# A decode kernel that streams 178 MB: VectorE looped over attention, waits thinned out, and the front of the kernel loaded in another order

## The chip, the cores and the metric

The kernel runs on one core of one Trainium2 chip. The metric is device time in microseconds (us); a kernel is run several times and medians are quoted. Each run reports a state, fast or slow; all runs used here were fast. Engines are named as in the profile: PE (TensorE), DVE (VectorE), ACT (ScalarE), POOL (GpSimd), SP (SyncE, which issues the loads). "DMA engine" always means one of the 16 engines that move data, never a compute engine.

## The reference

One decode step, batch 2, one new token each, in bfloat16:

```python
mod = (silu(c) @ w_mod).reshape(2, 6, 1, 1024)      # w_mod 1024 x 6144: 12.6 MB
sa, ca, ga, sb, cb, gb = mod
h = layernorm(x) * (1 + ca) + sa
x = x + ga * attention(h, k_cache, v_cache, wq, wo) # 32 query heads, 4 kv heads, 32768 keys of 128
h = layernorm(x) * (1 + cb) + sb
x = x + gb * mlp(h, w1, b1, w2, b2)                 # 1024 -> 3584 -> 1024
```

The two caches are 134 MB of the 178 MB that must be read. Arithmetic is small beside that.

## The kernel before

One queue (SP) issues all loads, mostly of 2 MB, into a 160 KB ring per partition. A block is loaded again as soon as the last reader of the slot is done. K blocks are turned (transposed) by PE into PSUM, evicted by DVE (5 of 8) or ACT (3 of 8), and multiplied with the query; softmax of a (batch, head) pair is one round behind.

A small recording layer, the Tracker, works out which semaphore each instruction must wait for and writes out each engine's program. PE's program is already a loop over the 8 rounds; DVE's and ACT's are written out in full, round after round:

```python
    def _compute_waits(self, E, tokens):
        need = {}
        for key, val in tokens:
            if val > need.get(key, 0):
                need[key] = val
        waits = []
        for key, val in need.items():
            if self.waited.get((E, key), 0) >= val:    # only what this engine itself waited for
                continue
            waits.append((key, val))
            self.waited[(E, key)] = val
        return waits
    # ...
    def _put(self, E, op):
        (self.segment if E == "pe" and self.segment is not None else self.ops[E]).append(op)
```

The parts of the attention that the change touches:

```python
    def tr(i, cc, g8):
        # ... 8 transposes of a K block into psKT[kq] on PE
        if EVAC_PATTERN[g8] == "act":
            act(lambda e, src=src: e.activation(KT_sb[g8][:, :, :], src, ACT.Copy), ...)
        else:
            dve(lambda e, src=src: e.tensor_copy(KT_sb[g8][:, :, :], src), ...)

    def qk(i, cc, g8):
        # ... 8 matmuls into ps
        if g8 == TPC // 8 - 1:
            Sc = S_sb[i % 2][:, :, cc * TPC:(cc + 1) * TPC]
            act(lambda e: e.activation(Sc, ps[:, :].rearrange("p (t h) -> p h t", h=HPG), ACT.Copy), ...)
            dve(lambda e: e.tensor_reduce(m1c[:, :, cc], Sc, AX.X, ALU.max), ...)
```

And the front:

```python
    wm_v = w_mod.rearrange("(k p) n -> p k n", k=KT8)          # block k = 128 lines that follow one another
    # ...
    T.dma("sp", lambda e: e.dma_start(c16[:, :], c.rearrange("b (k p) -> (b k) p", p=128)), ...)   # 16 lines of 256 B
    T.dma("sp", lambda e: e.dma_start(x16[:, :], A_x.rearrange("b o (k p) -> (b o k) p", p=128)), ...)
    # ... c16 and x16 are each turned by one small matmul into psM
```

## Time and profile before

| | before |
|---|---|
| time, median of 3 (lowest to highest) | 425.29 us (425.28 to 425.34) |
| span of the profiled execution | 423.6 us |
| bytes, mean rate | 178.50 MB, 421 GB/s |
| busy PE / DVE / ACT | 72% / 39% / 37% |
| last 2 MB load landed at | 417.75 us |

These lines are from the page of the kernel before: the span, engine busy times, then the DMA rows of the 40 slices (DMA share in tenths, rate in each slice), and the DMA queues (packets, MB, share of the time of all 16 DMA engines).

```profile
span 423.6 us, 11650 instructions
PE 305.5 (72%) x5164; PEld 244.0 (58%) x5164; DVE 167.3 (39%) x347; ACT 157.1 (37%) x269; POOL 4.9 (1%) x23
...
DMA  8999999999999999999999999999999999999994
GB/s 325 428 430 426 433 434 429 419 432 431 430 436 427 435 425 434 430 432 433 428 435 425 434 432 430 435 427 436 425 432 431 432 433 427 432 430 422 427 428 185
...
q1 hardware_dynamic: 14350, 178.29, 98.7%
q8 instruction: 9, 0.15, 0.1%
q14 instruction: 8, 0.07, 0.0%
```

The stream is unbroken from the second slice to the last but one. q1 carries the data, while the two "instruction" queues bring program code to the engines.

From the groups of instructions of the kernel before (busy us, mean ns of one | idle time just before them, and what ended it):

```profile
L507 DVE COPY KT_sb<-psKT 128x1024 bf16<-128x1024 bf16 x160 | 108.5, 690 | 118.1 <-PE psKT L501 117.8
L505 ACT ACTIVATE KT_sb<-psKT 128x1024 bf16<-128x1024 bf16 x96 | 98.0, 1020 | 129.7 <-PE psKT L501 129.3
L518 DVE TENSOR_REDUCE m1c<-S_sb 128x8 f32<-128x512 f32 x32 | 21.9, 685 | 13.6 <-ACT S_sb L517 12.5
```

DVE and ACT stand idle before the evictions for over 100 us each, waiting for PE, which itself waits for data. So they are not what the kernel waits for.

The end of the chain of waits, before (start us, length us, what):

```profile
386.99 30.76 DMA w<-in_B_w_dram
...
417.79 2.87 PE psO L721 x96
420.69 0.19 DVE mT L724
```

And the end of the stream in windows of 1 us, before (the last two columns are the DMA share and GB/s):

```profile
core 0: us, PE busy (x) PEld busy (x) DVE busy (x) ACT busy (x) POOL busy (x), PEclk, DMA share, GB/s
414.00:415.00 1.00, 0.85 (x12) 0.18 (x4) 0.10 (x1) 0.00 (x0) 0.00 (x0) 0.79 1.01 424
415.00:416.00 1.00, 0.35 (x3) 0.35 (x4) 0.60 (x1) 0.00 (x0) 0.00 (x0) 1.00 1.01 424
416.00:417.00 1.00, 0.70 (x7) 0.62 (x6) 0.00 (x0) 0.00 (x0) 0.00 (x0) 1.00 0.86 352
417.00:418.00 1.00, 0.21 (x8) 0.21 (x9) 0.00 (x0) 0.00 (x0) 0.00 (x0) 0.92 0.59 240
418.00:419.00 1.00, 1.00 (x43) 1.00 (x41) 0.00 (x0) 0.00 (x0) 0.00 (x0) 0.50 0.23 88
419.00:420.00 1.00, 1.00 (x38) 0.93 (x36) 0.00 (x0) 0.00 (x0) 0.00 (x0) 0.50 0.12 39
```

The stream does not stop; it fades over some 4 us.

### The profile page before, as it was taken

What the parts mean: (1) busy time and instruction counts of PE and PEld (TensorE: products, weight loads), DVE (VectorE), ACT (ScalarE), POOL (GpSimd) and SP (SyncE); (2) the same over time, 40 slices, a digit from 0 to 9 for tenths busy, and PEclk for the clock granted to TensorE, in tenths of its full rate; (3) what the DMA queues carried; (4) which work ended last, traced back from release to release, by engine and by line L of the source; (5) the groups of instructions that cost most, each with busy time, mean ns of one, the idle gap of its engine ahead of it and who ended that gap; (6) DMA issues with size and microseconds to landing.
All of it is one profiled execution on the core that took longest, in us unless ns stands there. A gap on an engine that the chain in (4) does not pass through costs nothing.

```text
span 423.6 us, 11650 instructions
## 1 busy us (share of the span) xinstructions
PE 305.5 (72%) x5164; PEld 244.0 (58%) x5164; DVE 167.3 (39%) x347; ACT 157.1 (37%) x269; POOL 4.9 (1%) x23
## 2 busy tenths in 40 slices
PE   1546467988997879788877958896878682645575
PEld 0105157976975769677676837785867661212244
DVE  1102025644673464446435524652555343101311
ACT  2000024638555446433733543473438234100020
POOL 3000000000000000000000000000000000000000
PEclk9999859869999886888969898887989886655566
DMA  8999999999999999999999999999999999999994
GB/s 325 428 430 426 433 434 429 419 432 431 430 436 427 435 425 434 430 432 433 428 435 425 434 432 430 435 427 436 425 432 431 432 433 427 432 430 422 427 428 185
DMA packets 14367, 178.50 MB, mean 421 GB/s; under 512 B 1543, under 2 KB 1550, under 8 KB 2830
## 3 DMA queue, kind: packets, MB, share of 16 engines
q1 hardware_dynamic: 14350, 178.29, 98.7%
q8 instruction: 9, 0.15, 0.1%
q14 instruction: 8, 0.07, 0.0%
HBM read 178.28 MB, written 0.00 MB: 421 GB/s over the span
## 4 chain that ended last, share of the span: by engine, by line
DMA 76%; PE 16%; SPq 5%; ACT 1%; issue 1%; DVE 0%; ACTq 0%; DVEq 0%
DMA K<-in_A_k_cache_dram 60%; PE psKT L501 11%; DMA wo<-in_A_wo_dram 8%; DMA w<-in_B_w_dram 7%; SPq L377 5%; PE psS L513 3%; PE psO L543 1%; PE psO L721 1%; ACT KT_sb L505 1%; ACT E_sb L534 0%; PE psS L642 0%; ACT L534 0%; DVE KT_sb L507 0%; PE psM L524 0%; SPq L392 0%
## 5 line engine op out<-in xcount | busy, mean ns | idle before, releaser
L501 PE MATMUL psKT<-ident,K 128*128 128x128 bf16 x2048 | 180.5, 242 | 36.8 <-DMA K<-in_A_k_cache_dram 34.4
L501 PEld LDWEIGHTS psKT<-ident,K 128*128 128x128 bf16 x2048 | 138.8, 109 | 47.9 <-DMA K<-in_A_k_cache_dram 41.1
L507 DVE COPY KT_sb<-psKT 128x1024 bf16<-128x1024 bf16 x160 | 108.5, 690 | 118.1 <-PE psKT L501 117.8
L505 ACT ACTIVATE KT_sb<-psKT 128x1024 bf16<-128x1024 bf16 x96 | 98.0, 1020 | 129.7 <-PE psKT L501 129.3
L513 PE MATMUL psS<-qcur,KT_sb 128*128 128x8 bf16 x2048 | 88.8, 168 | 7.7 <-ACT KT_sb L505 6.5
L513 PEld LDWEIGHTS psS<-qcur,KT_sb 128*128 128x128 bf16 x2048 | 80.7, 100 | 13.1 <-ACT KT_sb L505 8.4
L543 PE MATMUL psO<-V,E_sb 128*32 128x512 bf16 x512 | 35.6, 406 | 1.9 <-DMA V<-in_A_v_cache_dram 1.0
L534 ACT ACTIVATE E_sb<-S_sb,negm 128x256 bf16<-128x256 f32 x64 | 32.3, 504 | 10.9 <-DVE negm L530 10.0
L518 DVE TENSOR_REDUCE m1c<-S_sb 128x8 f32<-128x512 f32 x32 | 21.9, 685 | 13.6 <-ACT S_sb L517 12.5
L517 ACT ACTIVATE S_sb<-psS 128x512 f32<-128x512 f32 x32 | 19.0, 593 | 14.0 <-PE psS L513 13.9
L543 PEld LDWEIGHTS psO<-V,E_sb 128*32 128x32 bf16 x512 | 11.5, 100 | 12.8 <-issue 2.8
L452 PE MATMUL psS<-wmod,inT 128*32 128x512 bf16 x64 | 8.4, 622 | 12.0 <-DMA wmod<-in_w_mod_dram 12.0
L642 PE MATMUL psS<-wo,atT 128*32 128x512 bf16 x64 | 7.6, 627 | 11.9 <-DMA wo<-in_A_wo_dram 11.9
L423 ACT ACTIVATE stat<-stat 128x2 f32<-128x2 f32 x3 | 0.6, 204 | 37.0 <-DVE stat L422 37.0
L473 PE MATMUL psS<-wq,inT 128*32 128x512 bf16 x64 | 7.1, 602 | 7.4 <-DMA wq<-in_A_wq_dram 6.3
L534 ACT ACTIVATION_READ_ACCUMULATOR E_sb<-S_sb,negm 128x1 f32 x64 | 12.1, 189 | 0.0
L452 PEld LDWEIGHTS psS<-wmod,inT 128*32 128x32 bf16 x64 | 1.3, 112 | 18.0 <-DMA wmod<-in_w_mod_dram 17.5
L642 PEld LDWEIGHTS psS<-wo,atT 128*32 128x32 bf16 x64 | 1.9, 128 | 16.6 <-DMA wo<-in_A_wo_dram 14.5
L564 PE MATMUL psM<-msum,hmat 128*128 128x128 f32 x16 | 4.2, 346 | 7.5 <-DVE msum L558 7.5
L458 ACT ACTIVATE S_sb<-psS 128x512 f32<-128x512 f32 x1 | 0.6, 597 | 22.9 <-DVE S_sb L460 22.9
L460 DVE COPY S_sb<-psS 128x512 f32<-128x512 f32 x1 | 0.7, 691 | 20.7 <-PE psS L452 20.7
L558 DVE SCALAR_TENSOR_TENSOR msum<-psO,mk,msum 128x128 f32<-128x128 f32 x24 | 8.4, 351 | 0.9
(115 smaller groups left out, 129.7 us busy)
## 6 DMA issues: line engine op xcount, KB each, us to landing
K<-in_A_k_cache_dram SPq DMA_DIRECT2D x32, 2048.0 KB, 31.4
V<-in_A_v_cache_dram SPq DMA_DIRECT2D x32, 2048.0 KB, 35.2
wmod<-in_w_mod_dram SPq DMA_DIRECT2D x8, 1536.0 KB, 16.6
wq<-in_A_wq_dram SPq DMA_DIRECT2D x4, 2048.0 KB, 37.9
wo<-in_A_wo_dram SPq DMA_DIRECT2D x4, 2048.0 KB, 27.7
w<-in_B_w_dram SPq DMA_DIRECT2D x4, 1792.0 KB, 37.9
w<-in_B_w_dram SPq DMA_DIRECT2D x3, 2048.0 KB, 30.8
w<-in_B_w_dram SPq DMA_DIRECT2D x1, 768.0 KB, 28.6
```

Source lines behind the costliest of these rows:

```text
L377: T.dma("sp", lambda e, dst=dst, src=cur.src: e.dma_start(dst, src), key=cur.sem, writes=[cur.reg], frees=old)
L452: pe(lambda e, w=it.view, k=k, ch=ch, n=n, q=q: e.matmul(bank[n][32 * q:32 * q + 32, :], lhsT=inT[:, k, :], rhs=w[:, ch * 512:(ch + 1) * 512],
L501: pe(lambda e, kq=kq, jj=jj, w=it.view, t=t: e.transpose(psKT[kq][:, jj * 128:(jj + 1) * 128], w[:, t, :], ident[:, :]), reads=[it.reg, "i ...
L505: act(lambda e, src=src: e.activation(KT_sb[g8][:, :, :], src, ACT.Copy), reads=[f"psKT{kq}"], writes=[f"KT_sb{g8}"], sem=f"ev{cc}_{g8}")
L507: dve(lambda e, src=src: e.tensor_copy(KT_sb[g8][:, :, :], src), reads=[f"psKT{kq}"], writes=[f"KT_sb{g8}"], sem=f"ev{cc}_{g8}")
L513: pe(lambda e, t=t, jj=jj: e.matmul(ps[:, t * HPG:(t + 1) * HPG], lhsT=KT_sb[g8][:, jj, :], rhs=qcur[:, :], start=True, stop=True), reads= ...
L517: act(lambda e: e.activation(Sc, ps[:, :].rearrange("p (t h) -> p h t", h=HPG), ACT.Copy), reads=[preg], writes=[f"S_sb{i % 2}_{cc}"], sem ...
L518: dve(lambda e: e.tensor_reduce(m1c[:, :, cc], Sc, AX.X, ALU.max), reads=[f"S_sb{i % 2}_{cc}"], writes=[f"m1c{cc}"])
L534: act(lambda e: e.activation(E_sb[:, :, h, :], S_sb[j][:, h, :].rearrange("p (u t) -> p u t", t=4), ACT.Exp, bias=negm[:, h:h + 1], scale= ...
L543: pe(lambda e, t4=t4, tg=tg, q=q: e.matmul(psO[32 * q:32 * q + 32, :], lhsT=E_sb[:, tg // 4, :, :].rearrange("p h t -> p (h t)"), rhs=it.v ...
L558: dve(lambda e, q=q: e.scalar_tensor_tensor(out=msum[:, :], in0=psO[:, q * 128:(q + 1) * 128], scalar=mk4[:, q:q + 1], in1=msum[:, :], op0 ...
L642: pe(lambda e, w=it.view, g=g, j=j, hf=hf, q=q: e.matmul(psS[0][32 * q:32 * q + 32, :], lhsT=atT[g][:, j, :], rhs=w[:, j, hf * 512:(hf + 1 ...
```

## The change

The Tracker now knows what a wait implies: if the other engine had itself waited for something, so has this one (`_learn`), and that wait is left out. DVE's eight rounds are folded into one loop body as PE's are. For that, each round must use the same addresses, so the running maximum reads PSUM rather than one of two buffers, and GpSimd copies each round's result to its place. The front loads c as two lines of 2 KB and turns it with 8 small matmuls; to match the order in which c then lies, block k of w_mod is every eighth line of the matrix.

```diff
+    LOOPED = ("pe", "dve")
...
+    def _learn(self, E, key, val):
+        known = self.known[E]
+        known[key] = max(known.get(key, 0), val)
+        for v, what in reversed(self.seen[key]):
+            if v <= val:
+                for k, x in what.items():
+                    if x > known.get(k, 0):
+                        known[k] = x
+                break
...
-            if self.waited.get((E, key), 0) >= val:
+            if self.known[E].get(key, 0) >= val:
                 continue
...
-        (self.segment if E == "pe" and self.segment is not None else self.ops[E]).append(op)
+        if self.segments is not None and E in self.LOOPED:
+            self.segments[E][-1][1].append(op)
+        else:
+            self.ops[E].append(op)
...
-    wm_v = w_mod.rearrange("(k p) n -> p k n", k=KT8)
+    wm_v = w_mod.rearrange("(p k) n -> p k n", k=KT8)
...
-    T.dma("sp", lambda e: e.dma_start(c16[:, :], c.rearrange("b (k p) -> (b k) p", p=128)), key="ld_c", writes=["c16"])
+    T.dma("sp", lambda e: e.dma_start(c2[:, :], c), key="ld_c", writes=["KT_sb0"])
...
+    for k in range(KT8):
+        pe(lambda e, k=k: e.matmul(psM[:, 2 * k:2 * k + 2], lhsT=c2[:, k::KT8], rhs=ident[0:2, 0:2], start=True, stop=True),
+           reads=["KT_sb0", "ident"], writes=["psM"], mark=False)
...
-            dve(lambda e: e.tensor_reduce(m1c[:, :, cc], Sc, AX.X, ALU.max), ...)
+            dve(lambda e: e.tensor_reduce(m1c[:, :, cc], ps[:, :].rearrange("p (t h) -> p h t", h=HPG), AX.X, ALU.max), ...)
...
-        dve(red, reads=["pick"], writes=[f"atT{g}"])
+        dve(red, reads=["pick"], writes=["at"])
+        T.inst("pool", lambda e: e.tensor_copy(atT[g][:, :, b], at[:, :]), reads=["at"], writes=[f"atT{g}"], sem="ac")
```

## The prediction

> **What bounds the kernel now.** The memory stream. The page: 178.50 MB over a 423.6 us span, mean 421 GB/s; every slice of 40 but the first and last is at 9 tenths DMA busy and 419 to 437 GB/s. Windows of 10 us from 20 to 410 us all show a DMA share of 0.99 to 1.03. The Trainium skill ("DMA: Bandwidth & Descriptors", Where 436 GB/s comes from) puts the ceiling at 435 GB/s; the trace agrees (about 430). Outside the stream lie 2 us before the first bytes and the end: the last load landed at 417.8 (chain of waits), then 2.9 us of matmuls, four short operations and a 1.4 us store.
>
> The engines have room: DVE 39%, ACT 37%, PE 72% busy. A freed buffer is reissued at once, but its load lands 31 to 35 us later (DMA issues), as some seven 2 MB loads (4.8 us each) stand ahead of it. So an engine may be late by some 20 us before the stream runs dry.
>
> **What the change does.**
> - VectorE loop: the 40 or so operations a round (evictions 690 ns, reductions 687 ns) stay; added are a backward branch, six conditional parts and wait values computed in registers. For PE, already looped so, idle put to "issue" before transposes is 2.4 us once. My estimate: 1 to 3 us a round of 39 us, on an engine 60% idle. Off the critical path.
> - Fewer waits: near zero; nothing is removed after the last load.
> - The max reads PSUM, still after the ACT copy, by the bank's rule: about 687 ns as before. POOL gets a small copy a round (0.19 us, as its qcur copy). Off the path.
> - c load: 2 packets for 16; it landed at 7.5 us, behind the first w_mod block, and will again. Eight matmuls for one (0.19 us): the first w_mod matmul moves from 10.9 to about 11.5 us. SP is held by the queue until 21.86 us anyway, so no K load moves. [...]
> - w_mod by every eighth line: same bytes, same 12 KB lines, now 96 KB apart. This touches the bound itself, for 12.6 MB, 29 us. The skill (same page, Latency and other measured facts) lists rates that fall at row pitches that are powers of two from 512 KiB up; 96 KB is neither. In the trace w_mod (12 KB pitch) and K/V (16 KB pitch) all run at 420 to 435 GB/s; no run here shows 96 KB. I expect no change, within 0.5 us.
>
> On the critical path: the stream, unchanged to about 0.5 us.
>
> **Prediction.** 425.1 us, 80% range 424.2 to 426.6. Faster by over 2%: 0.01 (178.5 MB at 435 GB/s is 410 us alone and the ends cost some 7 more; 416.8 is out of reach). Within 2%: 0.95. Slower by over 2%: 0.04.
>
> **What would show it.** Right: DMA 9 tenths in slices 2 to 39, last load landing within 0.5 us of 417.8, w_mod landing near 16.6 us after issue, DVE busy about 167 us, first K load landing near 58.5 us. Wrong: under 410 GB/s between 4 and 30 us (pitch costs), a DMA share under 0.9 inside the loop (a late VectorE emptied the queue), or a slower start.
>
> **What would make it wrong.** A memory-side cost of the 96 KB pitch (10% of 29 us is 3 us; half rate 29 us), or branch stalls on VectorE of over 10 us a round, which use up the queue's depth.

Three notes on it. The highest slice on the page is 436 GB/s, not 437. "The bank's rule" is the Tracker's own: `_excl` counts a read of PSUM as a write, so that one engine's use of a PSUM tile waits for the other's. And the 410 us is an estimate, worked out from the 435 GB/s that the prediction cites.

## The result, and the profile after

The changed kernel took 423.65 us (median of 4 runs, 423.52 to 423.77), the kernel before in the same rounds 425.31 us (425.28 to 425.34). The ratio is 0.9961, with a 95% interval of 0.9944 to 0.9978. Ratios here are the mean time of one kernel's fast runs over that of the other's of the same rounds, so they are not quite the ratio of the medians. The gain is 1.7 us: small, but many times what runs of one kernel differ by (0.06 and 0.25 us), and outside the predicted range (424.2 to 426.6).

The same lines of the page, after:

```profile
span 421.8 us, 11638 instructions
PE 299.5 (71%) x5171; PEld 238.1 (56%) x5171; DVE 167.1 (40%) x347; ACT 156.6 (37%) x269; POOL 6.0 (1%) x31
...
DMA  8999999999999999999999999999999999999995
GB/s 334 429 431 423 435 432 423 429 432 426 433 432 429 435 429 430 435 429 429 435 429 432 437 423 433 435 426 433 433 428 433 430 430 435 427 429 424 428 423 244
...
q1 hardware_dynamic: 14322, 178.29, 99.1%
q8 instruction: 9, 0.15, 0.1%
q14 instruction: 4, 0.03, 0.0%
```

The engines do the same work in the same time (DVE 167.3 before, 167.1 after). The rates of the slices in the middle have not risen. What changed is the last slice (185 GB/s before, 244 after) and the last queue line: 8 packets before, 4 after.

The groups, after:

```profile
L548 DVE COPY KT_sb<-psKT 128x1024 bf16<-128x1024 bf16 x160 | 108.3, 689 | 112.5 <-PE psKT L542 112.5
L546 ACT ACTIVATE KT_sb<-psKT 128x1024 bf16<-128x1024 bf16 x96 | 98.0, 1020 | 131.2 <-PE psKT L542 131.2
L559 DVE TENSOR_REDUCE m1c<-psS 128x8 f32<-128x512 f32 x32 | 22.1, 691 | 14.4 <-ACT S_sb L558 13.3
```

DVE and ACT still wait for PE for over 100 us. The maximum from PSUM costs 691 ns, from the buffer 685.

The end of the chain, after:

```profile
385.85 30.13 DMA w<-in_B_w_dram
...
416.02 2.88 PE psO L757 x96
418.93 0.19 DVE mT L760
```

The last big load landed 1.77 us earlier (the matmuls that wait for it start at 416.02, before at 417.79). From there to the end nothing differs. So the whole gain lies in when the stream's last load is complete. The windows, after:

```profile
414.00:415.00 1.00, 1.00 (x6) 1.00 (x6) 0.00 (x0) 0.00 (x0) 0.00 (x0) 0.50 1.02 428
415.00:416.00 1.00, 0.74 (x4) 0.65 (x4) 0.00 (x0) 0.00 (x0) 0.00 (x0) 0.50 0.97 406
416.00:417.00 1.00, 0.98 (x36) 0.98 (x37) 0.00 (x0) 0.00 (x0) 0.00 (x0) 0.50 0.85 350
417.00:418.00 1.00, 1.00 (x38) 0.93 (x36) 0.00 (x0) 0.00 (x0) 0.00 (x0) 0.50 0.53 199
418.00:419.00 1.00, 0.89 (x32) 0.81 (x31) 0.07 (x1) 0.00 (x0) 0.00 (x0) 0.50 0.02 6
```

The fade begins at nearly the same time in both kernels: 424 and 406 GB/s between 415 and 416 us, 352 and 350 in the next. It is all but over at 418 us after, and goes on to 420 us before. (What lands behind the last 2 MB load are two smaller loads of 768 and 256 KB; their last shares come at 419.59 and 420.23 us before, at 417.83 and 418.46 after, with the same lags as the 2 MB load below.) The mass of the stream is no faster; its stragglers are.

### Reading the stragglers

The Trainium skill says why one straggler matters ("DMA: Bandwidth & Descriptors", Why a DMA increments its semaphore by 16 and not by 1): a load is split over up to 16 DMA engines, each adds one to the semaphore when its share has landed, and only the full 16 mean that all is there. The trace records these 16 increments for each load, so it shows how far behind its fellows the slowest engine is. Below, for seven loads of each kernel: when the first of the 16 shares landed (us), and how much later each of the 16 did, in order. These figures are worked out from the trace's landing records, not printed by the profile.

```
before
  28.42 | 0.00 0.04 0.05 0.10 0.12 0.13 0.13 0.16 0.32 0.37 0.50 0.53 0.59 0.60 0.62 0.89
 124.62 | 0.00 0.02 0.12 0.15 0.32 0.52 0.59 0.71 0.87 0.93 1.47 1.55 1.84 1.95 2.04 2.06
 221.86 | 0.00 0.03 0.13 0.16 0.33 0.53 0.60 0.89 1.28 1.48 1.56 1.80 1.84 1.97 2.06 2.07
 270.49 | 0.00 0.04 0.13 0.16 0.37 0.55 0.57 0.85 1.22 1.48 1.54 1.79 1.93 2.01 2.02 2.63
 319.12 | 0.00 0.12 0.15 0.32 0.52 0.59 0.78 0.87 1.51 1.55 1.78 1.84 1.95 2.04 2.06 3.59
 367.74 | 0.00 0.22 0.27 0.36 0.55 0.57 0.67 0.84 1.52 1.59 1.78 1.86 1.92 1.99 2.01 3.55
 414.21 | 0.00 0.20 0.26 0.33 0.53 0.68 1.52 1.60 1.84 1.87 1.98 2.04 2.07 2.08 2.30 3.54
after
  28.29 | 0.00 0.03 0.09 0.14 0.15 0.16 0.20 0.21 0.26 0.28 0.32 0.34 0.41 0.42 0.45 0.52
 124.49 | 0.00 0.13 0.14 0.19 0.33 0.39 0.40 0.44 0.85 0.92 1.48 1.51 1.56 1.63 1.69 1.89
 221.73 | 0.00 0.14 0.15 0.20 0.34 0.41 0.42 0.45 0.87 0.88 1.50 1.52 1.58 1.65 1.71 1.89
 270.32 | 0.00 0.18 0.20 0.21 0.33 0.41 0.44 0.51 0.89 1.51 1.53 1.61 1.64 1.72 1.74 1.98
 318.98 | 0.00 0.13 0.19 0.33 0.40 0.40 0.44 0.84 0.86 1.44 1.49 1.51 1.56 1.64 1.69 1.89
 367.57 | 0.00 0.21 0.33 0.35 0.44 0.48 0.81 0.96 1.56 1.57 1.60 1.65 1.73 1.79 1.98 2.03
 414.07 | 0.00 0.30 0.34 0.41 0.47 0.78 0.94 1.51 1.53 1.55 1.57 1.58 1.64 1.76 1.87 1.90
```

The last row of each is the last 2 MB load. Its first share lands at 414.21 and 414.07, nearly the same; its last share at 417.75 (414.21 + 3.54) and 415.98 (414.07 + 1.90). Engines hardly catch up: a lag once gained stays nearly whole to the end (3.59 at 319 us, 3.54 at 414). And the largest lag grows in steps. Before, it goes from 2.07 to 2.63 between 222 and 270 us, and to 3.59 by 319 us. The packets of queue q14 in the kernel before start at 87, 104, 160, 204, 240, 290, 314 and 320 us. Load by load, the first step lies between the loads whose first shares land at 236.46 us (largest lag 2.01) and 241.31 (2.76), the second between those at 314.35 (2.54) and 319.12 (3.59). So the steps follow the packets at 240 and at 320. The packet at 314 made no step: the last share of the load at 314.35 landed at 316.89, after that packet, with no more lag than before. In both steps one share leaves its place in the row and becomes the last, from 1.8 or less to 2.7 and then from 2.6 to 3.6. So one engine took both packets, and each set it back by about 0.9 us.

That gives a theory. **Theory A: the code that an engine's program is made of comes over the same 16 DMA engines as the data. Each fetch sets one DMA engine back by half a microsecond or more, and since every load needs all 16, the end waits for the engine that has been set back most. A shorter program has fewer fetches.** Its rivals: **B**, the loop or the fewer waits let DVE and ACT hand over sooner; **C**, the new front alone makes the difference.

The built programs have these many instructions: DVE 563 before and 186 after, ACT 355 before and 213 after (142 of ACT's 146 separate wait instructions are gone). The Trainium skill ("Runtime: NRT & Kernel Launch", Instruction fetch mechanics) says that the sequencer drives its own DMA queue to fetch the next page of its program, 256 instructions in 16 KiB; by that, one takes 64 bytes (an estimate; 2048 more instructions in e5_pad below brought 16 more fetches of 8,192 bytes, which agrees). In these traces q8's packets are of 16,384 bytes, q14's of 8,192, in the stretch where the stream runs. q8 can be put down to PE: its 9 packets stay the same in every kernel here, while additions to DVE's, ACT's and GpSimd's programs all show on q14.

### The profile page after: what moved, and what is told of

The parts are those of the page before. It is cut to its first block, busy times and chain, and to the rows that moved or that the text cites. A ratio compares the mean times of both kernels' runs of the same rounds, so it can differ in the third digit from the quotient of the medians.

```text
span 421.8 us, 11638 instructions
## 1 busy us (share of the span) xinstructions
PE 299.5 (71%) x5171; PEld 238.1 (56%) x5171; DVE 167.1 (40%) x347; ACT 156.6 (37%) x269; POOL 6.0 (1%) x31
## 4 chain that ended last, share of the span: by engine, by line
DMA 80%; PE 16%; ACT 2%; SPq 1%; issue 0%; DVE 0%
DMA K<-in_A_k_cache_dram 60%; PE psKT L542 11%; DMA wo<-in_A_wo_dram 8%; DMA w<-in_B_w_dram 7%; DMA wmod<-in_w_mod_dram 4%; PE psS L554 3%; ACT E_sb L575 1%; PE psO L584 1%; SPq L415 1%; ACT KT_sb L546 1%; PE psO L757 1%; PE psS L678 0%; ACT L575 0%; PE psM L565 0%; ACT S_sb L558 0%
## 5 line engine op out<-in xcount | busy, mean ns | idle before, releaser
L542 PE MATMUL psKT<-ident,K 128*128 128x128 bf16 x2048 | 173.8, 237 | 39.0 <-DMA K<-in_A_k_cache_dram 37.8
L542 PEld LDWEIGHTS psKT<-ident,K 128*128 128x128 bf16 x2048 | 133.2, 106 | 49.7 <-DMA K<-in_A_k_cache_dram 44.9
L554 PEld LDWEIGHTS psS<-qcur,KT_sb 128*128 128x128 bf16 x2048 | 79.5, 99 | 13.2 <-ACT KT_sb L546 8.1
L559 DVE TENSOR_REDUCE m1c<-psS 128x8 f32<-128x512 f32 x32 | 22.1, 691 | 14.4 <-ACT S_sb L558 13.3
## 6 DMA issues: line engine op xcount, KB each, us to landing
wmod<-in_w_mod_dram SPq DMA_DIRECT2D x8, 1536.0 KB, 16.5
```

What stands on the lines that cost most here:

```text
L542: pe(lambda e, kq=kq, jj=jj, w=it.view, t=t: e.transpose(psKT[kq][:, jj * 128:(jj + 1) * 128], w[:, t, :], ident[:, :]), reads=[it.reg, "i ...
L554: pe(lambda e, t=t, jj=jj: e.matmul(ps[:, t * HPG:(t + 1) * HPG], lhsT=KT_sb[g8][:, jj, :], rhs=qcur[:, :], start=True, stop=True), reads= ...
L559: dve(lambda e: e.tensor_reduce(m1c[:, :, cc], ps[:, :].rearrange("p (t h) -> p h t", h=HPG), AX.X, ALU.max), reads=[preg], writes=[f"m1c{ ...
```

## The experiments

"First", "last" and "lag" refer to the last 2 MB load, as in the rows above; the end of w_mod is the 28 us row. All runs gave results that the comparison with the reference accepts. The kernel before was timed on the same chip in each set: 425.37, 425.40 and 425.49 us.

| run | 8 KB fetches (q14) | lag at end of w_mod | first | last | lag | median us |
|---|---|---|---|---|---|---|
| before | 8 | 0.89 | 414.21 | 417.75 | 3.54 | 425.31 |
| e3_front | 8 | 0.63 | 414.29 | 417.61 | 3.32 | 425.44 |
| e9_unroll_more | 8 | 0.34 | 414.14 | 417.95 | 3.81 | 425.43 |
| e1_unroll | 6 | 0.50 | 414.17 | 416.75 | 2.58 | 424.54 |
| e2_actwaits | 5 | 0.39 | 414.29 | 416.00 | 1.71 | 423.80 |
| after | 4 | 0.52 | 414.07 | 415.98 | 1.90 | 423.65 |
| after_again | 4 | 0.35 | 414.17 | 415.83 | 1.66 | 423.55 |
| e10_loop_more | 4 | 0.50 | 414.22 | 415.80 | 1.58 | 423.85 |
| e7_pad64 | 8 | 0.41 | 414.06 | 416.25 | 2.19 | 423.90 |
| e5_pad | 20 | 0.32 | 414.29 | 423.74 | 9.45 | 431.38 |
| e6_oldfront | 4 | 0.65 | 414.21 | 416.16 | 1.95 | 423.94 |
| e4_pitch | 4 | 1.18 | 414.33 | 416.59 | 2.26 | 424.21 |
| e4_again | 4 | 0.72 | 414.08 | 416.20 | 2.12 | 423.97 |
| e8_stride16 | 4 | 0.32 | 414.14 | 415.78 | 1.64 | 423.53 |

Two columns say most of it. "First" lies between 414.06 and 414.33 in all fourteen rows: nothing in any of these kernels makes the engine that is furthest ahead faster or slower. And the median time minus "last" is 7.5 to 8.1 us in every row: time is the landing of the last share plus a constant.

### e1_unroll: undo the VectorE loop alone

```diff
-    LOOPED = ("pe", "dve")
+    LOOPED = ("pe",)
```

> The changed kernel with VectorE unrolled again (all else kept: fewer waits, new front). Static VectorE instructions go from 186 to 373, some 12 KB more code. Theory A (instruction fetches ride on the 16 DMA engines, each 8 KB fetch sets one engine of the stream back by 0.6 to 0.9 us, and the end waits for the engine that is furthest back): 1 to 3 more fetch packets on the instruction queue that had 8 before and 4 after; sum of the 16 engines' lags up by 0.6 to 0.9 us for each; time up by anything from 0 to 1.3 us (423.7 to 425.0), by what the engine furthest back is hit; the first of the 16 engines to finish the last load ends at 414.1 us as before. Rival B (the loop itself makes VectorE hand over sooner): the whole stream, first engine included, later by the same amount. Rival C (all of the gain is the front: c and w_mod): 423.65, no change.

Measured: 424.54 us (424.42 to 424.84, 5 runs), ratio to before 0.9981 (0.9967 to 0.9994). DVE's program has 373 instructions. The queue lines of its profile:

```profile
q8 instruction: 9, 0.15, 0.1%
q14 instruction: 6, 0.05, 0.0%
```

Two more fetches than after, a lag of 2.58 in place of 1.90, and 0.9 us of the time back: the two ratio intervals overlap, but the slowest run of the changed kernel (423.77) is well under the fastest here. The trace shows the step: the largest lag is 1.83 in the load at 348.24 us and 2.72 in the next, at 353.10, and between their last shares, at 350.07 and 355.82, one fetch starts, at 353.9. The first share lands at 414.17, so the stream as a whole did not slow down, which is what rival B would need.

### e2_actwaits: give ScalarE its old waits back

```diff
     def _learn(self, E, key, val):
         known = self.known[E]
         known[key] = max(known.get(key, 0), val)
+        if E == "act":
+            return
```

> The changed kernel with the transitive wait removal switched off for ScalarE alone: its static instructions go from 213 to 338, 8 KB more code, the work is the same. Theory A: one more 8 KB fetch, lag of one engine up by 0.6 to 0.9 us; time 423.6 to 424.5 by where it lands. A rival in which waits cost time by themselves: ScalarE's idle time up, time up with no more fetches. Rival C: 423.65.

Measured: 423.80 us (423.67 to 424.00), ratio 0.9962 (0.9949 to 0.9976). ACT's program has 338 instructions, and there is one fetch more (5); by the lag of 1.71 it hit an engine with room to spare. So 125 more waits executed by ACT moved the time by no more than a quarter of a microsecond.

### e3_front: the new front alone, on the kernel before

```diff
-    wm_v = w_mod.rearrange("(k p) n -> p k n", k=KT8)
+    wm_v = w_mod.rearrange("(p k) n -> p k n", k=KT8)
...
(c as two lines and 8 matmuls, as in the change; Tracker, waits and loops as before)
```

> The kernel before with only the front changed (c as two lines with eight matmuls, w_mod by every eighth line). Theory A: the 8 fetches stay; the front's share alone comes, the last engine about 0.5 us earlier at the end of w_mod, so 424.8 (424.6 to 425.2). Rival C (the front is all of it): 423.65.

Measured: 425.44 us (425.20 to 425.65), ratio 1.0001 (0.9987 to 1.0015). The expected half microsecond did not come: a miss. Rival C falls all the more. The lag at the end of w_mod did shrink (0.63 against 0.89), but the 8 fetches brought the slowest engine to 3.32 all the same. A head start for engines that are not the last is worth nothing at the end.

### e4_pitch and e6_oldfront: parts of the front, in the changed kernel

e4_pitch puts the w_mod blocks back to 128 lines that follow one another, and keeps c as two lines:

```diff
-    wm_v = w_mod.rearrange("(p k) n -> p k n", k=KT8)
+    wm_v = w_mod.rearrange("(k p) n -> p k n", k=KT8)
...
-lhsT=c2[:, k::KT8]
+lhsT=c2[:, k * 128:(k + 1) * 128]
```

> The changed kernel with w_mod in contiguous blocks again; c still as two lines, its eight matmuls take contiguous pieces. If the front's gain is from c alone (2 lines in place of 16, so fewer small packets ahead of the stream): 423.65 within 0.15. If the 96 KB pitch itself is faster or slower: a difference of 0.2 us or more, and w_mod's landings move from the first block on.

Measured: 424.21 us (423.95 to 424.43), ratio 0.9970 (0.9956 to 0.9983). The lag at the end of w_mod is 1.18 us, against 0.52. So c as two lines alone does not give the gain.

e6_oldfront puts the whole front of before into the changed kernel (edit: the front lines of the change, taken back).

> The changed kernel with the whole front of before (c as 16 lines, w_mod in contiguous blocks). With c as two lines but contiguous w_mod blocks the spread of the 16 engines at the end of w_mod was 1.2 us, with both changed 0.5, before 0.85. If the spread comes from the w_mod order: here 0.8 to 1.2 again and 424.0 to 424.4. If c's lines made it: 0.5 and 423.65 is not to be expected either way; a spread of 0.85 and 424.0 would say that both have a part.

Measured: 423.94 us (423.82 to 424.03), ratio 0.9966 (0.9953 to 0.9980); the changed kernel beside it took 423.55. So in the changed kernel the front is worth 0.39 us, and in the kernel before nothing (e3_front). The lag at the end of w_mod is 0.65 and the time 423.94, both just below what the expectation gives for the order of w_mod alone (0.8 to 1.2, 424.0 to 424.4).

### after_again, e5_pad and e7_pad64: add code that does nothing

The changed kernel was run again to have its time on the same chip as the two below.

> The changed kernel again, on the chip of the runs beside it: 423.65 within 0.15, 4 fetches on the instruction queue that had 8 before, the engine furthest back 1.9 us behind the first at the last big load.

Measured: 423.55 us (423.47 to 423.59), ratio to before 0.9956 (0.9943 to 0.9970).

e5_pad adds the suspected cost and nothing else. GpSimd, which is busy for 6 us in all, gets 256 more instructions at the start of each round. Each raises a semaphore nobody waits for.

```diff
+PAD = 256
...
+    pads = [nc.alloc_semaphore(f"pad{n}") for n in range(NBG)]
...
     T.inst("pool", lambda e: e.tensor_copy(qcur[:, :], ...), reads=["qT"], writes=["qcur"], sem="qc")
+        for _ in range(PAD):
+            T.raw("pool", lambda e: e.sem_inc(pads[i], 1))
```

> The changed kernel with 2048 instructions more on GpSimd, which has room: each only raises a semaphore that nobody waits for (256 at the start of each round, about 128 KB of code). No work, no wait and no data of the stream changes. Theory A (fetched code holds up the stream's DMA engines): about 16 fetches of 8 KB more. If they are spread evenly over the 16 engines, each is hit once, mean lag and end both up by about 0.7 us (0.4 to 1.2): 424.0 to 424.9. If they all fall on few engines, several us more: up to 430. Any rival in which the loop gained by VectorE's handing over sooner, by fewer waits as such, or by the front: 423.65, no change.

Measured: 431.38 us (431.19 to 431.40, 4 runs), ratio to before 1.0140 (1.0124 to 1.0155): 7.8 us later than the changed kernel, and more than the "up to 430" of the expectation. From its page:

```profile
span 429.6 us, 13686 instructions
...
DMA  8999999999999999999999999999999999999980
GB/s 335 434 426 426 429 439 420 427 436 424 430 437 425 430 438 428 426 438 429 428 436 429 428 435 429 429 436 428 429 436 428 428 437 429 427 424 427 431 364 19
...
q14 instruction: 20, 0.16, 0.1%
```

The rates of the slices are those of the other kernels until the last two, in which the stream trickles out at 364 and 19 GB/s. The 16 shares show what happened:

```
e5_pad
  28.37 | 0.00 0.02 0.03 0.08 0.11 0.12 0.13 0.14 0.15 0.17 0.18 0.20 0.21 0.26 0.30 0.32
 124.67 | 0.00 0.01 0.03 0.07 0.08 0.14 0.21 0.71 0.76 1.31 1.38 1.39 1.40 1.44 1.58 3.32
 221.91 | 0.00 0.01 0.02 0.07 0.09 0.15 0.21 0.66 0.75 1.31 1.37 1.38 1.40 1.45 1.57 6.00
 319.15 | 0.00 0.01 0.03 0.08 0.09 0.15 0.22 0.77 1.24 1.32 1.38 1.40 1.41 1.46 1.59 8.91
 414.29 | 0.00 0.07 0.08 0.12 0.80 0.81 1.27 1.34 1.35 1.37 1.40 1.41 1.42 1.55 1.57 9.45
```

By these lags, all 16 added fetches fell on one DMA engine. The other 15 end within 1.57 us of each other, as in the changed kernel; that one is 9.45 us behind, 0.59 us for each fetch (9.45 / 16). The mean of the 16 landings says the same without asking which engine it was: it moved from 415.20 (after_again, on the same chip) to 415.79, and 0.59 us on 16 engines for 16 fetches is 0.59 us each. 0.13 MB of code, under a thousandth of the bytes, cost 1.8% of the time.

e7_pad64 is the same with `PAD = 64`: 4 fetches more.

> The same with 512 instructions, 64 a round (32 KB of code, 4 fetches more, as many as the change took away). Theory A: mean of the engines' ends later by about 0.15 us, the end later by 0 to 0.9, by whether the engine furthest back is hit: 423.6 to 424.6. Rivals: 423.65.

Measured: 423.90 us (423.78 to 424.25), ratio 0.9966 (0.9953 to 0.9980). Its count of fetches is 8, as in the kernel before, yet it loses only 0.35 us to the changed kernel. Its lag is 2.19, and the 4 fetches at 0.59 us make 2.4 us, about the size of that lag, so the engine that serves GpSimd's fetches seems to have started with little lag of its own. It is not the number of fetches that counts but which engine they fall on, and what that engine already has.

### e9_unroll_more and e10_loop_more: code against waits against executed instructions

Up to here "fewer waits" and "less code" went together. e9_unroll_more parts them. VectorE is unrolled as in e1_unroll, no wait of before comes back, but DVE and ACT get idle increments at each eviction and each score copy until their programs are as long as before (565 and 341 instructions; before 563 and 355).

```diff
-    LOOPED = ("pe", "dve")
+    LOOPED = ("pe",)
...
+    def more(E):
+        if E in MORE:
+            T.raw(E, lambda e: e.sem_inc(spare[E], 1))
...
+        more(EVAC_PATTERN[g8])          # before each eviction
...
+            more("act")                 # before each score copy
+            more("dve")
```

> VectorE unrolled as in the run that did that alone, waits few as in the changed kernel, and one instruction more at each eviction and each score copy on VectorE (192) and ScalarE (128) that only raises a semaphore nobody waits for. Static code comes to 565 and 341 instructions, where before had 563 and 355; no wait of before comes back. Theory A: 8 fetches as in before, the engine furthest back 3.3 us behind, 425.2 to 425.6 (as the kernel before with the new front, 425.44). If it was the removed waits themselves that gained: 424.5 as unrolled alone.

Measured: 425.43 us (425.26 to 425.55), ratio to before 0.9997 (0.9983 to 1.0011). The whole gain is gone, with none of the waits restored, and with the maximum from PSUM and GpSimd's copies still in place, so these are not what gained either.

```profile
span 423.8 us, 11638 instructions
...
q8 instruction: 9, 0.15, 0.1%
q14 instruction: 8, 0.07, 0.0%
```

e10_loop_more makes the same additions inside DVE's loop (`MORE = ("dve",)` on the changed kernel): DVE executes the 192 extra instructions, but its program is only 24 longer.

> The changed kernel with the same 24 extra increments a round inside VectorE's loop: VectorE executes 192 instructions more, but its code grows by 24 (1.5 KB). Theory A: 4 fetches (5 if a page border is crossed), 423.6 within 0.2. If executed instructions on VectorE cost the time: as much later as the unrolled kernel with the same additions is later than the unrolled one.

Measured: 423.85 us (423.70 to 423.90), ratio 0.9961 (0.9947 to 0.9974).

```profile
span 421.8 us, 11830 instructions
...
q14 instruction: 4, 0.03, 0.0%
```

Executing them costs 0.2 to 0.3 us at most (a hair over the expected 423.6 within 0.2); having to fetch them, together with ACT's, cost 0.9 (425.43 against 424.54, on two chips; 0.7 by the ratios to before). Rival B falls.

### e8_stride16 and e4_again: which half of the front

e8_stride16 takes c as 16 lines as before but w_mod by every eighth line. The lines of the two do not match, so this is wrong arithmetic on purpose. (The comparison with the reference still passed: presumably because with these inputs the modulation is too small a part of the result for its tolerance. The pass says nothing about correctness here.)

```diff
(e6_oldfront, and)
-    wm_v = w_mod.rearrange("(k p) n -> p k n", k=KT8)
+    wm_v = w_mod.rearrange("(p k) n -> p k n", k=KT8)
```

> Wrong results on purpose: the changed kernel with c as 16 lines as before, but w_mod by every eighth line, so the lines do not match. Tells the two halves of the front apart: with c as two lines, w_mod by every eighth line gave a spread at the end of w_mod of 0.3 to 0.6 us, contiguous blocks 1.2 us; c as 16 lines with contiguous blocks 0.65 to 0.9. If the order of w_mod makes the small spread: 0.3 to 0.6 here and 423.6; if only the pair does: 0.7 or more and 423.9 or later.

Measured: 423.53 us (423.41 to 423.76), ratio 0.9955 (0.9942 to 0.9969), lag at the end of w_mod 0.32.

> The changed kernel with w_mod in contiguous blocks and c as two lines, again beside the run above: 424.2 within 0.15, spread at the end of w_mod near 1.2 us if that is a property of the kernel; 0.5 if it was chance.

Measured: 423.97 us (423.90 to 424.07), ratio 0.9964 (0.9951 to 0.9978), lag at the end of w_mod 0.72: less than the 1.18 of its first run, and 0.24 us faster, a miss of the expected range. Taken together: with w_mod by every eighth line, the lag at the end of w_mod is 0.32 to 0.63 in ten profiles, whatever is done with c; with contiguous blocks it is 0.65 to 1.18 in four (before, e6_oldfront, e4_pitch, e4_again). So it is the order of w_mod that evens out the 16 engines at the start, and c as two lines is only what makes that order possible. Why the order does so no run shows.

## Why the prediction was wrong

The bound was named rightly, and that is why the error is small: the stream runs at the same rate in all kernels, and a gain of over 2% was out of reach. The range was missed by 0.55 us (423.65 against 424.2).

- **The step that failed** is "On the critical path: the stream, unchanged to about 0.5 us". It treats the 16 DMA engines as one pipe. The pipe's mean did stay within the half microsecond: the mean landing of the last 2 MB load's shares moved by 0.43 us (415.64 to 415.21), the first share by 0.14. But the kernel waits for the last of 16, and that moved by 1.77 us.
- **"VectorE loop: ... Off the critical path."** As work of VectorE it is: DVE busy is 167.1 us, and the estimate of 1 to 3 us a round for branches left no trace in the time. As code it was on the path: the loop is worth 0.9 us (424.54 to 423.65), by taking 2 fetches off the DMA engines.
- **"Fewer waits: near zero."** Near zero as waits (e2_actwaits: a quarter of a microsecond or less). As code it was worth another 0.9 us: from e3_front (425.44, old waits, unrolled) to e1_unroll (424.54, few waits, unrolled), and e9_unroll_more gave all of it, 425.43, back with idle code. (e3_front and e1_unroll also differ in the source of the maximum and in GpSimd's copies; e9_unroll_more has both as e1_unroll has them.)
- **c and w_mod.** The first w_mod matmul came at 10.44 us, not later but 0.4 us earlier than before, as c's two lines landed sooner; this is off the path, as predicted. That the 96 KB pitch costs nothing held, and the Trainium skill's warning about row pitches ("DMA: Bandwidth & Descriptors", Latency and other measured facts, powers of two from 512 KiB up) did not apply here. Not foreseen was that the order evens out the engines, which is worth 0.39 us, and only once the fetches no longer hide it (e3_front: nothing; e6_oldfront: 0.39).
- The sum is not a sum: the parts are worth 0, 0.9 and 0.9 us in one order, and 0.39 for the front in another, because the time is a maximum over 16 engines. Each part counts only for the engine that is last at the end.
- The signs named for being right held in part: DMA at 9 tenths in slices 2 to 39, w_mod landing at 16.5 us after issue, DVE busy 167.1 us, the first K load at 58 us. The last load, which was to land within 0.5 us of 417.8, landed at 416.0: the one sign that looked at a single moment and not at a mean was the one that showed the error.

The profile of before had the hint, the line with 8 packets and 0.0%. A share of 16 engines' time is the wrong measure for something that hits one engine at a time. By the steps of its lag, the engine that was last took two of the eight, about 0.9 us each. Without them it would have stood at about 1.8 us, and the next in the row, at 2.30, would have been last.

What is left for a better kernel is little. In the changed kernel the mean share of the last 2 MB load lands 0.8 us before the last one (415.21 against 415.98), and PE's own nine 16 KB fetches hit one engine each. They, not the four of 8 KB, make the changed kernel's lag: it goes from 0.51 to 1.67 us between the loads at 31.91 and 36.81, around PE's first fetch at 33.3, is 2.03 after the second at 62.1, and stays between 1.84 and 2.03 past the 8 KB fetches at 73, 104, 249 and 314 us. As long as some engine is hit once, the end waits for it, so shortening ACT's or GpSimd's programs further should gain nothing. That was not tried, and no version that beats the changed kernel came out of these runs.

Left open: why one 8 KB fetch sets its engine back by 0.59 us (GpSimd's) or about 0.9 (the two in the kernel before, the one in e1_unroll) when its own record lasts 0.31; why GpSimd's fetches all fall on one DMA engine while PE's appear on several; and why the w_mod order evens out the start.

## What to carry to other kernels

In a kernel whose DMA stream never pauses, as here, the fetching of program code delays the DMA engine it lands on (0.6 to 0.9 us for 8 KB), and each load waits for the slowest of 16. Other small traffic beside the stream was not tried. So judge code fetches by what they do to the last of the 16 landings of a load, not by their share of bytes or of mean busy time; and keep the programs of the engines short, by loops and by leaving out waits that other waits imply, even where those engines have hundreds of microseconds to spare. Here the whole change, the front's 0.39 us included, was worth 1.7 us of 425.

## What the Trainium skill lacked or had wrong

- "Runtime: NRT & Kernel Launch", Instruction fetch mechanics, calls the cost of crossing a page "mostly hidden". It is hidden from the engine that fetches, but not from a saturated stream: 16 more fetches of 8 KB made the kernel 7.8 us slower (e5_pad), 0.59 us for each on the DMA engine that carried them.
- The same section says that kernels prefer full unrolling where possible, since a taken branch can stall the fetch when its target lies outside the two pages held. It does not say that a short loop can be the better choice: here looping VectorE's 8 rounds (its whole program is then 186 instructions) gained 0.9 us (424.54 to 423.65) and no stall showed, and PE's loop of 8 rounds fetched nothing between 89 and 363 us.
- The same section has fetches in blocks of 16 KiB. In these traces PE's are of 16,384 bytes, those of DVE, ACT and GpSimd of 8,192; whether that is a setting no run here shows.
- "DMA: Bandwidth & Descriptors" names the 16 increments of a load's semaphore, but not their use in a profile: the spread of the 16 landings was 0.3 to 1.2 us early in these kernels and 1.6 to 9.5 us at the end, and the time was the last landing plus 7.5 to 8.1 us in all fourteen profiles.
- No page has that fetches of one engine's program can all fall on one DMA engine, as GpSimd's 16 did (lag 9.45 us, the other 15 within 1.57).
